# First batch of an attention + ELU MLP kernel: more places for softmax weights and raw weight words, earlier weight loads, v read once

## The chip, the cores and the metric

The kernel runs on one core of one Trainium2 chip. The metric is device microseconds of one execution.

## The reference

Eight batches of 12 heads with 448 positions and 64 channels go through attention with RMS-normalised q and k; the result, 3584 tokens of 768 channels, goes through a two-layer MLP with ELU and 2048 hidden channels. All in float32.

```python
q_n, k_n = rmsnorm(q, g_q), rmsnorm(k, g_k)
scores = q_n @ k_n.T / sqrt(64)
attn = exp(scores - max); attn = attn / (sum(attn) + 1e-09)
x = (attn @ v)                      # (8, 12, 448, 64) -> (3584, 768)
h = x @ w_in                        # (3584, 2048)
g = where(h > 0, h, exp(min(h, 0)) - 1)
return g @ w_out                    # (3584, 768)
```

## The kernel before

**Number format.** Products run on TensorE in float16. Each operand is split into a high and a low float16 part and scaled by powers of two; a product is three matmuls (high x high, high x low, low x high). For the weights this splitting is done once, on the chip, by `conv_in` (16 blocks f of `w_in`, results `whi[f]`, `wli[f]`) and `conv_out` (24 blocks of `w_out`, results `who[d]` and, through DRAM, `wl_d`). The power for v needs the largest absolute value of a batch's v: `scan_load` brings v in six pieces, `scan_max` (L139, DVE) takes the maxima, `v_steps` joins them.

**Tiling.** Two heads make a pair, six pairs a batch, 48 pairs in all. A pair has 7 chunks of 128 query rows (`T` counts chunks, 42 a batch, 336 in all). Per chunk: `s_mm` (L488, PE) computes scores into PSUM, `s_max` (L495, DVE) the row maxima, `s_exp` (L501, ACT), `s_z` (POOL), `s_rec` (DVE), then `s_hi` (L516, ACT) writes the softmax weights' high half into a buffer `p16`, `s_lo` (L522, DVE) the low half, and `s_tr` (L533) issues a transposing DMA `pt<-p` on the SP queue. `p16` has three buffers, so chunk T+3's `s_hi` waits until chunk T's transposes have landed. After its seven chunks a pair's `attend` (L544, PE) multiplies with v. `load_qk` (L307), `load_v` (L311, one buffer `vn`) and `qk_transpose` (L396) prepare later pairs on the same SP queue.

**MLP.** `mlp(b)` is 576 matmuls (L630, L644) per batch, spread over the half-steps of the next batch. So in the first batch no MLP matmul runs; the conversion of `w_in` fills that time, `w_out`'s begins in half-step 60 and ends in the second batch.

**Order.** The order is written out: a half-step `h` (two for a chunk, 84 for a batch, from -18 on) runs its loads first, then the chunk's softmax steps, then the tasks put down for it with `at`, then matmuls. Each engine works through its instructions in this order, and so does the SP queue, which issues every DMA; an SP instruction that waits holds back all behind it.

**Raw words.** `conv` starts a block f of `w_in` with `load` (L187, 768 KB), one half-step ahead of its h0, into one of two places of `raws`; `s_act` (L194, L195, ACT) reads it at h0+3, `s_sign` (L223, DVE) is the last reader at h0+7. Three blocks come every 14 half-steps, that is every pair (h0 = -10 + 14*((f-1)//3) + 0, 5 or 10). The blocks of `w_out` (512 KB) go through three places of the same tile.

Of the kernel before, what the change touches and what calls it, by code (L numbers as in the profile page):

```python
# [8 lines left out]
F32 = mybir.dt.float32  # L9
F16 = mybir.dt.float16  # L10
BF16 = mybir.dt.bfloat16
I32 = mybir.dt.int32
U32 = mybir.dt.uint32
# [6 lines left out]
B, H, S, D = 8, 12, 448, 64  # L20
NPAIR = H // 2
DM, DFF = 768, 2048
NC_, NF = DM // 128, DFF // 128
NJ = 2 * S // 128
NCHUNK = B * NPAIR * NJ
PB = NPAIR * NJ
WI_W, WO_W = DM, 32 * NF
# [5 lines left out]
def tile_attention_then_elu_mlp(ctx: ExitStack, tc: tile.TileContext, qk, v, v_scan, gg, w_in, w_out, out):  # L33
# [13 lines left out]
    nc = tc.nc  # L47
    nc.scalar.preload_act_table_set("natural_log_exp_and_others")

    const = ctx.enter_context(tc.tile_pool(name="const", bufs=1))  # L50
    dram = ctx.enter_context(tc.tile_pool(name="dram", bufs=1, space=DRAM))
    psum = ctx.enter_context(tc.tile_pool(name="psum", bufs=1, space=PSUM))
    pool = ctx.enter_context(tc.tile_pool(name="pool", bufs=1))
# [9 lines left out]
    def t_mo():  # L63
        return pst("mo", 3)
# [7 lines left out]
        out=neg, in0=ident, scalar1=-1.0, scalar2=None, op0=ALU.mult  # L72
# [3 lines left out]
        out=ident, in0=ident, scalar1=2.0**UP, scalar2=None, op0=ALU.mult  # L76
# [3 lines left out]
    eps = const.tile([128, 1], F32, name="eps")  # L80
    nc.vector.memset(eps, 1e-6)

    wl_d = [dram.tile([128, 128, NF], F16, name=f"wl_d{d}") for d in range(NC_)]

    whi = [const.tile([128, NC_, 128], F16, name=f"whi{f}") for f in range(NF)]
    wli = [const.tile([128, NC_, 128], F16, name=f"wli{f}") for f in range(NF)]
    who = [const.tile([128, 128, NF], F16, name=f"who{d}") for d in range(NC_)]
    NX = 9
    xs = [const.tile([128, 2, S], F16, name=f"x{i}") for i in range(NX)]
    gts = [const.tile([128, 2, S], F16, name=f"g{f}") for f in range(NF)]  # L90

    raws = const.tile([128, 2 * 2 * WI_W], U32, name="raws")
    wts = const.tile([128, 2 * WI_W], F32, name="wts")
    w32s = const.tile([128, 3 * WI_W], F32, name="w32s")

    def room(all, width, i):
        n = all.shape[1] // width
        return all[:, i % n * width : i % n * width + width]  # L100

    def small(name, w=1, dt=F32, bufs=2):
        return pool.tile([128, w], dt, tag=name, name=name, bufs=bufs)
# [3 lines left out]
    def upper(t):  # L107

        return t.bitcast(BF16).rearrange("p (n w) -> p n w", w=2)[:, :, 1]

    def column_sums(parts, bank):


        for i, a in enumerate(parts + [tiny]):
            nc.tensor.matmul(bank[:, S:], ones, a, start=i == 0, stop=i == len(parts))

    def largest(bank, e):
        nc.vector.tensor_reduce(out=e, in_=bank[:, S:], axis=AX.X, op=ALU.max)  # L118
        return e
# [3 lines left out]
    def ibits(dst, src, s1, op0, s2, op1):  # L123
        nc.vector.tensor_scalar(
            out=dst.bitcast(I32), in0=src.bitcast(I32), scalar1=s1, scalar2=s2, op0=op0, op1=op1
        )

    E = 1 << 23

    scans, mvs = {}, {}  # L130

    def scan_load(b, i):
        raw = scans[b, i] = pool.tile([128, VSW], F32, tag="e", name="vscan", bufs=3)
        nc.sync.dma_start(out=raw, in_=v_scan[b][:, i * VSW : (i + 1) * VSW])

# [30 lines left out]
    def on_pe(fn):  # L166

        late.add(fn)
        return fn
# [6 lines left out]
    def conv(src, i, width, acol, rows, parts, own=True):  # L176

        raw = room(raws, 2 * width, i).rearrange("p (n w) -> p n w", w=2)

        t, w = room(wts, width, i), room(w32s, width, i if width == WI_W else i + 2)
        ws = bank = None

        def load():
            nc.sync.dma_start(  # L187
                out=raw, in_=src[i].bitcast(U32).rearrange("p (n w) -> p n w", w=2)
            )

        def s_act():


            nc.scalar.activation(t, raw[:, :, 1].bitcast(F32), AF.Abs, scale=2.0**-112)  # L194
            nc.scalar.activation(w.bitcast(I32), raw[:, :, 0], AF.Copy, scale=2.0**-29)  # L195

        def s_shift():
            nc.vector.tensor_scalar(  # L198
                out=t.bitcast(I32), in0=t.bitcast(I32), scalar1=3, scalar2=None,
                op0=ALU.logical_shift_left,  # L200
            )

        def s_add():
            nc.gpsimd.tensor_tensor(
                out=w.bitcast(I32), in0=t.bitcast(I32), in1=w.bitcast(I32), op=ALU.add
            )

        def s_sums():
            nonlocal bank
            bank = t_mo() if own else av  # L210
            column_sums([upper(t[:, a : a + 64]) for a in range(0, width, 64)], bank)

        def s_scale():
            nonlocal ws
            e = largest(bank, acol if rows is None else small("mx"))
            ws = small("ws")

            ibits(ws, e, POWER, ALU.bitwise_xor, POWER, ALU.bitwise_and)
            if rows is not None:
                ibits(acol, e[rows], POWER, ALU.bitwise_and, 0, ALU.bitwise_or)  # L220

        def s_sign():
            nc.vector.scalar_tensor_tensor(  # L223
                out=w.bitcast(U32), in0=raw[:, :, 1], scalar=0x80000000, in1=w.bitcast(U32),
                op0=ALU.bitwise_and, op1=ALU.bitwise_or,
            )

        steps = [
            (0 if (width, i) == (WO_W, 1) else -1, load), (3, s_act), (4, s_shift), (5, s_add), (6, on_pe(s_sums)), (7, s_sign),
            (8, s_scale),  # L230
        ]
        for h, fn in parts:
            step = lambda fn=fn: fn(w, ws)
            steps.append((h, on_pe(step) if fn in late else step))
        return steps

    def conv_in(f):
        hi, lo = (t[f].rearrange("p c n -> p (c n)") for t in (whi, wli))
        half = [slice(0, 384), slice(384, 768)]
        dgw = None  # L240
        pss = [None, None]

        def s_diag(w, ws):
            nonlocal dgw
            dgw = pool.tile([128, 128], F32, tag="dgw", name="dgw", bufs=2)
            nc.scalar.activation(dgw, ident, AF.Copy, scale=ws)

        def s_high(w, ws):
            nc.gpsimd.tensor_scalar(
                out=hi, in0=w, scalar1=ws, scalar2=2.0**UP, op0=ALU.mult, op1=ALU.mult  # L250
            )

        def s_low(w, ws):
            for i, c in enumerate(half):
                pss[i] = t_mo()
                nc.tensor.matmul(pss[i][:, :384], dgw, w[:, c], start=True, stop=False)
                nc.tensor.matmul(pss[i][:, :384], neg, hi[:, c], start=False, stop=True)

        def s_out(i):
            nc.scalar.activation(lo[:, half[i]], pss[i][:, :384], AF.Copy)  # L260

        return conv(
            w_in, f, WI_W, a_in[:, f : f + 1], None,
            [(9, s_diag), (9, s_high), (11, on_pe(s_low)), (12, lambda w, ws: s_out(0)),
             (13, lambda w, ws: s_out(1))],
        )
# [31 lines left out]

    nat, vn, vt, qkt, pts, pss, p16s, stats = ({} for _ in range(8))
    st1, sqs, t16s = {}, {}, {}
    vscale, mscale, vpow = {}, {}, {}

# [2 lines left out]
        nc.sync.dma_start(out=nat[p].rearrange("p t j d -> p (t j) d"), in_=qk[p // NPAIR, p % NPAIR])  # L307

    def load_v(p):
        vn[p] = pool.tile([128, 4, 2, D], F32, tag="vn", name="vn", bufs=1)  # L310
        nc.sync.dma_start(out=vn[p], in_=v[p // NPAIR, p % NPAIR])  # L311

# [199 lines left out]
        nc.vector.reciprocal(out=st[:, 2:3], in_=st[:, 1:2])  # L512

    def s_hi(T):
        p16 = p16s[T] = pool.tile([128, 2 * S], F16, tag="p16", name="p16", bufs=3)
        nc.scalar.activation(p16[:, :S], pss[T][:, :S], AF.Copy, scale=stats[T][:, 2:3])  # L516

    def s_lo(T):
# [143 lines left out]
    def run_tasks(h, kind):  # L662
        for fn, args in tasks.get(h, []):
            if kind == (0 if fn in (load_qk, load_v, scan_load) else 2 if fn in late else 1):
                fn(*args)
# [24 lines left out]
    for b in range(B):  # L690
        h0 = HB * (b - 1) + HP * 2 if b else -5
        for i in range(VSC):
            at(h0 + 2 * i, scan_load, b, i)
            at(h0 + 2 * i + 3, scan_max, b, i)
        steps_at(h0 + (15 if b else 13), v_steps(b))
        at(HB * (b + 1), m_scale, b)
# [23 lines left out]
    for h in range(H0, LAST):  # L720
        T, odd = divmod(h, 2)
        run_tasks(h, 0)
        ok = lambda t: 0 <= t < NCHUNK
        if odd:
            if ok(T):
                s_exp(T)
            if ok(T - 1):
                s_rec(T - 1)
            if ok(T - 2):
                s_lo(T - 2)  # L730
        else:
            if ok(T):
                s_max(T)
            if ok(T - 1):
                s_z(T - 1)
            if ok(T - 2):
                s_hi(T - 2)

            for t in (T - 4, T - 3):
                if ok(t) and (t % NJ == 0) == (t == T - 4):  # L740
                    s_tr(t)
        run_tasks(h, 1)
        want = int(max(0, (h + 1 - START)) * RATE)
        n = max(0, want - done)
        mm = []
        p, r = divmod(h, HP)
# [15 lines left out]
    h = LAST - 1  # L762
# [49 lines left out]
```

## Time and profile before

| | |
|---|---|
| median of 3 runs | 1323.66 us (1322.05 to 1326.17) |
| profiled execution, its time | 1321.52 us |
| its span | 1319.7 us |
| mean granted TensorE clock | 0.957 |
| busy: PE, DVE, ACT, POOL | 1202.7, 897.0, 820.8, 672.4 us |

The profile's page cuts the span into 40 slices of 33 us and gives busy tenths for each engine, the granted TensorE clock (PEclk) and the busy share of the 16 DMA engines:

```profile
PE   3665558879999999999999999999999999999998
PEclk9777768989999999999999999999999999999999
DMA  7899998879878787888878877879687877764011
```

TensorE is at 9 tenths from the tenth slice on; the first slices are the first batch, and the second batch's start.

### The profile page before, as it was taken

The numbers are of one execution on the slowest core, as the hardware profiler recorded it, in microseconds if no ns is written. First come the engines' busy times: TensorE is split into PE (matmuls) and PEld (weight loads), VectorE is DVE, ScalarE is ACT, GpSimd is POOL, SyncE is SP. The second block draws the span as 40 slices with busy tenths as digits, with TensorE's granted clock in tenths as the row PEclk, the third lists the DMA queues.
The fourth block names the chain that finished last, engine by engine and source line by source line (L and its number), as shares of the span: only waits on it lengthen the run. The fifth ranks groups of instructions, "written<-read, shape, count | busy, mean of one in ns | idle before, by whom it ended". The sixth has DMA issues, their size and how long they took to land.

```text
span 1319.7 us, 22020 instructions
## 1 busy us (share of the span) xinstructions
PE 1202.7 (91%) x6976; PEld 723.1 (55%) x6976; DVE 897.0 (68%) x2257; ACT 820.8 (62%) x1761; POOL 672.4 (51%) x915
## 2 busy tenths in 40 slices
PE   3665558879999999999999999999999999999998
PEld 1322224436755675566655765577556755666576
DVE  7776788988668756885588657865687568842310
ACT  5767767776667657675577657756676567742310
POOL 5776798888445544544455345543454445421100
PEclk9777768989999999999999999999999999999999
DMA  7899998879878787888878877879687877764011
GB/s 236 195 233 223 201 203 189 209 205 204 199 140 194 163 187 151 178 165 189 173 153 177 190 172 147 187 171 193 144 190 163 189 150 154 152 135 110 1 46 60
DMA packets 491013, 221.76 MB, mean 168 GB/s; under 512 B 451856, under 2 KB 467344, under 8 KB 490896
## 3 DMA queue, kind: packets, MB, share of 16 engines
q1 hardware_dynamic: 490896, 220.35, 75.6%
q8 instruction: 55, 0.90, 0.3%
q14 instruction: 62, 0.51, 0.1%
HBM read 96.01 MB, written 14.16 MB: 83 GB/s over the span
## 4 chain that ended last, share of the span: by engine, by line
PE 67%; DMA 4%; DVE 4%; POOL 2%; issue 2%; ACT 2%; SPq 0%; ACTq 0%; POOLq 0%
PE mo L644 32%; PE mo L630 22%; PE s L488 7%; PE av L544 6%; DMA pt<-p 2%; DMA vscan<-in_v_scan 1%; DVE p L522 1%; POOL e L571 1%; POOL t L381 1%; DVE st L495 1%; DVE mv L139 0%; DVE e L577 0%; ACT p L516 0%; DVE wts L198 0%; ACT t L367 0%
## 5 line engine op out<-in xcount | busy, mean ns | idle before, releaser
L630 PE MATMUL mo<-x,whi 128*128 128x448 f16 x1536 | 425.8, 354 | 1.5 <-DVE e L577 1.5
L644 PE MATMUL mo<-g,who 128*128 128x448 f16 x1536 | 422.5, 352 | 0.0
L495 DVE TENSOR_REDUCE st<-s 128x1 f32<-128x448 f32 x336 | 208.1, 619 | 205.5 <-PE s L488 205.3
L522 DVE SCALAR_TENSOR_TENSOR p<-s,st,p 128x384 f16<-128x384 f32 (+1 forms) x672 | 266.4, 437 | 34.7 <-ACT p L516 33.2
L516 ACT ACTIVATE p<-s,st 128x448 f16<-128x448 f32 x336 | 213.1, 634 | 120.7 <-DMA pt<-p 95.3
L644 PE MATMUL mo<-g,wls 128*128 128x448 f16 x768 | 272.0, 354 | 0.0
L630 PE MATMUL mo<-x,wli 128*128 128x448 f16 x768 | 271.8, 354 | 0.0
L644 PEld LDWEIGHTS <-who 128*128 128x128 f16 x1536 | 221.9, 144 | 72.3
L505 POOL TENSOR_SCALAR st<-st 128x1 f32<-128x1 f32 x336 | 78.6, 234 | 350.7 <-ACT s L501 333.5
L501 ACT ACTIVATE s<-s,st 128x448 f32<-128x448 f32 x336 | 203.8, 607 | 74.0 <-DVE st L495 64.6
L488 PE MATMUL s<-qkt 128*128 128x448 f16 (+1 forms) x768 | 191.4, 372 | 58.9 <-DVE p L522 30.7
L630 PEld LDWEIGHTS <-whi 128*128 128x128 f16 x1536 | 150.6, 98 | 139.6 <-issue 4.4
L571 POOL TENSOR_SCALAR e<-e,isc 128x448 f32<-128x448 f32 x128 | 94.1, 735 | 179.5 <-ACT e L568 177.7
L644 PEld LDWEIGHTS <-wls 128*128 128x128 f16 x768 | 111.5, 145 | 42.1 <-issue 7.5
L488 PEld LDWEIGHTS <-qkt 128*128 128x128 f16 (+1 forms) x768 | 61.3, 102 | 131.6 <-DVE p L522 52.2
L544 PE MATMUL av<-pt,vt 128*64 128x448 f16 x1056 | 114.6, 366 | 5.2 <-DVE mx L118 4.3
L585 DVE SCALAR_TENSOR_TENSOR g<-e,gsc,g 128x448 f16<-128x448 f32 x128 | 100.8, 788 | 24.4 <-ACT g L582 24.3
L630 PEld LDWEIGHTS <-wli 128*128 128x128 f16 x768 | 75.2, 98 | 74.5 <-issue 8.1
L582 ACT ACTIVATE g<-e,gsc 128x448 f16<-128x448 f32 x128 | 85.4, 667 | 44.9 <-DVE e L577 44.1
L568 ACT ACTIVATE e<-mo,sc 128x448 f32<-128x448 f32 x128 | 80.4, 628 | 52.3 <-PE mo L630 33.1
L381 POOL TENSOR_TENSOR t<-nat,t 128x896 f16<-128x896 f32 x48 | 92.7, 1931 | 4.8 <-ACT t L367 1.1
L577 DVE SCALAR_TENSOR_TENSOR e<-e,mo 128x448 f32<-128x448 f32 x128 | 78.2, 611 | 23.9 <-POOL e L571 19.3
(84 smaller groups left out, 1330.0 us busy)
## 6 DMA issues: line engine op xcount, KB each, us to landing
wls<-wl_d SPq DMA_DIRECT2D x48, 512.0 KB, 3.9
nat<-in_qk SPq DMA_DIRECT2D x48, 448.0 KB, 3.7
raws<-in_w_in SPq DMA_DIRECT2D x16, 768.0 KB, 5.5
vn<-in_v SPq DMA_DIRECT2D x48, 256.0 KB, 3.7
raws<-in_w_out SPq DMA_DIRECT2D x24, 512.0 KB, 4.2
vscan<-in_v_scan SPq DMA_DIRECT2D x48, 224.0 KB, 3.0
out<-y SPq DMA_DIRECT2D x48, 224.0 KB, 3.2
pt<-p SPq DMA_TRANSPOSE x384, 3.2
```

The costliest lines, as they stand in the source:

```text
L381: nc.gpsimd.tensor_tensor(out=t[:, 2], in0=twice(nat[p][:, 1]), in1=t[:, 1], op=ALU.subtract)
L488: nc.tensor.matmul(ps[r0 : r0 + n, :S], lhs, qq[:, t, h * S : h * S + S], start=(t == 1), stop=(t == 2),)
L495: nc.vector.tensor_reduce(out=st[:, 0:1], in_=pss[T][:, :S], axis=AX.X, op=ALU.max, negate=True)
L501: nc.scalar.activation(ps, ps, AF.Exp, bias=st[:, 0:1], accum_out=st[:, 1:2])
L516: nc.scalar.activation(p16[:, :S], pss[T][:, :S], AF.Copy, scale=stats[T][:, 2:3])
L522: nc.vector.scalar_tensor_tensor(out=p16[:, o : o + z - a], in0=ps[:, a:z], scalar=r, in1=p16[:, a:z], op0=ALU.mult, op1=ALU.subtract,)
L544: nc.tensor.matmul(av[64 * h : 64 * h + 64, :S], vt[p][:, j % 4, h, i], pt[h][:, j, :], start=(k == 0), stop=(k == len(terms) - 1),)
L571: nc.gpsimd.tensor_scalar(out=e, in0=e, scalar1=-1.0, scalar2=isc, op0=ALU.add, op1=ALU.mult)
L582: nc.scalar.activation(g[:, 0], e, AF.Copy, scale=gsc)
L585: nc.vector.scalar_tensor_tensor(out=g[:, 1], in0=e, scalar=gsc, in1=g[:, 0], op0=ALU.mult, op1=ALU.subtract)
L630: nc.tensor.matmul(ph[:, :S], w[:, c, :], x[:, r, :], start=(c == 0 and i == 0), stop=last)
L644: nc.tensor.matmul(py[:, :S], w, g[:, r, :], start=(f == 0 and i == 0), stop=last)
```

## The change

- The scan of the first batch reads v in the layout that `attend` needs: `scan_load` brings pair i's v (256 KB) into `vfirst[i]`, which lies in the MLP's later `g` tiles (`gall`), and keeps it; `load_v` issues nothing for the first six pairs. The separate scan loads (6 x 224 KB) of batch 0 are gone.
- `s_hi` of the first 42 chunks uses eight places, `pfirst`, in the other half of `gall`, instead of three pool buffers.
- `conv_in` has six places for raw words: the two of `raws` and four in `whos`, the tile that `who` is now part of. Its load is issued 1 half-step ahead of h0 for block 2, 4 for block 3 and 7 for the later ones. (Blocks 0 and 1 have their own table and stay.)

```diff
+    whos = const.tile([128, NC_ * 128 * NF], F16, name="whos")
+    who = [t.rearrange("p (n f) -> p n f", f=NF) for t in cols(whos, NC_)]
...
+    gall = const.tile([128, NF * 2 * S], F16, name="gall")
+    gts = [t.rearrange("p (i s) -> p i s", i=2) for t in cols(gall, NF)]
+    vfirst = cols(gall[:, : NPAIR * 1024].bitcast(F32), NPAIR)
+    pfirst = cols(gall, NF)[8:]
...
+    raw_in = cols(raws, 2) + cols(whos.bitcast(U32), 4)
...
     def scan_load(b, i):
+        if b == 0:
+            scans[b, i] = vfirst[i]
+            vn[i] = vfirst[i].rearrange("p (j h d) -> p j h d", j=4, h=2)
+            nc.sync.dma_start(out=vn[i], in_=v[0, i])
+            return
...
-        raw = room(raws, 2 * width, i).rearrange("p (n w) -> p n w", w=2)
+        raw = raw_in[i % len(raw_in)] if width == WI_W else room(raws, 2 * width, i)
+        raw = raw.rearrange("p (n w) -> p n w", w=2)
...
-            (0 if (width, i) == (WO_W, 1) else -1, load), (3, s_act), (4, s_shift), ...
+            (-(1, 4, 7)[min(max(i - 2, 0), 2)] if width == WI_W else 0 if i == 1 else -1, load), (3, s_act), (4, s_shift), ...
...
     def load_v(p):
+        if p < NPAIR:
+            return
...
     def s_hi(T):
+        if T < PB:
+            p16 = p16s[T] = pfirst[T % len(pfirst)]
+        else:
+            p16 = p16s[T] = pool.tile([128, 2 * S], F16, tag="p16", name="p16", bufs=3)
```

On the compute engines the instructions stand as before, with other tiles. What moves is the SP queue. At the program's start, before (`raws` is a place for raw words, `vscan` a piece of the scan, `vn` a pair's v, `nat` a pair's q and k, `qkt<-t` their transposes):

```order
L187 DMA raws<-in_w_in 128x1536
L134 DMA vscan<-in_v_scan 128x448
L307 DMA nat<-in_qk 128x896
L134 DMA vscan<-in_v_scan 128x448
L311 DMA vn<-in_v 128x512
L134 DMA vscan<-in_v_scan 128x448
L187 DMA raws<-in_w_in 128x1536
L134 DMA vscan<-in_v_scan 128x448 x2
L187 DMA raws<-in_w_in 128x1536
L134 DMA vscan<-in_v_scan 128x448
L396 DMA_TRANSPOSE qkt<-t_308 128x7x128 x2
```

The same place after (`whos` holds raw words, `gall` pairs' v):

```order
L205 DMA whos<-in_w_in 128x1536
L148 DMA gall<-in_v 128x512
L205 DMA whos<-in_w_in 128x1536
L325 DMA nat<-in_qk 128x896
L148 DMA gall<-in_v 128x512
L205 DMA whos<-in_w_in 128x1536
L148 DMA gall<-in_v 128x512 x2
L205 DMA whos<-in_w_in 128x1536
L148 DMA gall<-in_v 128x512 x2
L416 DMA_TRANSPOSE qkt<-t_283 128x7x128 x2
```

Four blocks of raw words instead of three now stand ahead of the second pair's transposes, the second and third of them earlier among the loads of v; the piecewise scan and the first `vn` are gone.

The end of the fourth pair (pair 3) on the SP queue, before (`pt<-p` are the softmax weights' transposes; the first two of a pair wait for the PE's `attend` of the pair ahead, whose `pt` buffers they take):

```order
L396 DMA_TRANSPOSE qkt<-t_1068 128x7x128 x2
L307 DMA nat<-in_qk 128x896
L533 DMA_TRANSPOSE pt<-p_1122 128x7x128
L533 DMA_TRANSPOSE pt<-p_1148 128x7x128
L396 DMA_TRANSPOSE qkt<-t_1068 128x7x128
L187 DMA raws<-in_w_in 128x1536
L533 DMA_TRANSPOSE pt<-p_1222 128x7x128
L311 DMA vn<-in_v 128x512
L533 DMA_TRANSPOSE pt<-p_1255 128x7x128
L187 DMA raws<-in_w_in 128x1536
```

And after:

```order
L416 DMA_TRANSPOSE qkt<-t_1015 128x7x128 x2
L205 DMA whos<-in_w_in 128x1536
L325 DMA nat<-in_qk 128x896
L556 DMA_TRANSPOSE pt<-gall 128x7x128 x2
L416 DMA_TRANSPOSE qkt<-t_1015 128x7x128
L556 DMA_TRANSPOSE pt<-gall 128x7x128 x2
```

The raw words that stood behind the two blocked transposes and the third `qkt` now stand ahead of them, the `vn` load is gone, and no further load of `w_in` follows in this stretch.

More of the change, by code (lines that the diff above doesn't have):

```diff
@@ L81, in tile_attention_then_elu_mlp, with cols @@
     nc.vector.memset(eps, 1e-6)
+    def cols(t, n):
+        w = t.shape[1] // n
+        return [t[:, i * w : i * w + w] for i in range(n)]
     wl_d = [dram.tile([128, 128, NF], F16, name=f"wl_d{d}") for d in range(NC_)]
@@ L86, in tile_attention_then_elu_mlp @@
     wli = [const.tile([128, NC_, 128], F16, name=f"wli{f}") for f in range(NF)]
-    who = [const.tile([128, 128, NF], F16, name=f"who{d}") for d in range(NC_)]
+    whos = const.tile([128, NC_ * 128 * NF], F16, name="whos")
+    who = [t.rearrange("p (n f) -> p n f", f=NF) for t in cols(whos, NC_)]
     NX = 9
     xs = [const.tile([128, 2, S], F16, name=f"x{i}") for i in range(NX)]
-    gts = [const.tile([128, 2, S], F16, name=f"g{f}") for f in range(NF)]
+    gall = const.tile([128, NF * 2 * S], F16, name="gall")
+    gts = [t.rearrange("p (i s) -> p i s", i=2) for t in cols(gall, NF)]
+    vfirst = cols(gall[:, : NPAIR * 1024].bitcast(F32), NPAIR)
+    pfirst = cols(gall, NF)[8:]
     raws = const.tile([128, 2 * 2 * WI_W], U32, name="raws")
@@ L128, in tile_attention_then_elu_mlp @@
     E = 1 << 23
-    scans, mvs = {}, {}
+    scans, mvs, vn = {}, {}, {}
     def scan_load(b, i):
+        if b == 0:
[3 more added lines that the diff above has]
+            return
         raw = scans[b, i] = pool.tile([128, VSW], F32, tag="e", name="vscan", bufs=3)
@@ L228, in conv @@
         steps = [
-            (0 if (width, i) == (WO_W, 1) else -1, load), (3, s_act), (4, s_shift), (5, s_add), (6, on_pe(s_sums)), (7, s_sign),
+            (-(1, 4, 7)[min(max(i - 2, 0), 2)] if width == WI_W else 0 if i == 1 else -1, load), (3, s_act), (4, s_shift), (5, s_add), (6, on_pe(s_sums)), (7, s_sign),
             (8, s_scale),
@@ L297, in conv_out @@
         )
-    nat, vn, vt, qkt, pts, pss, p16s, stats = ({} for _ in range(8))
+    nat, vt, qkt, pts, pss, p16s, stats = ({} for _ in range(7))
     st1, sqs, t16s = {}, {}, {}
@@ L514, in s_hi @@
     def s_hi(T):
-        p16 = p16s[T] = pool.tile([128, 2 * S], F16, tag="p16", name="p16", bufs=3)
+        if T < PB:
+            p16 = p16s[T] = pfirst[T % len(pfirst)]
+        else:
+            p16 = p16s[T] = pool.tile([128, 2 * S], F16, tag="p16", name="p16", bufs=3)
         nc.scalar.activation(p16[:, :S], pss[T][:, :S], AF.Copy, scale=stats[T][:, 2:3])
```

## The prediction

> **What bounds the kernel now.** I read the page's slices first (shown above): TensorE is full from the tenth slice on, so only what shortens the first 300 us can shorten the run. Then busy time by stretches. I cut them at every seventh row maximum (L495), so each stretch is one pair of heads; that work is the same in each, as the first two rows, of L495 alone, show for the first and the last (x7, one for each chunk). The other rows are the six pairs of the first batch, two pairs of the second batch, and one of the steady part. Columns: length, busy us and instructions of PE, PEld, DVE, ACT, POOL, then granted clock, DMA busy share, GB/s.
>
> ```profile
> 24.00:48.00 24.00, 4.30 (x7) 0.84 0.87 229
> 153.50:180.00 26.50, 4.25 (x7) 0.63 0.92 216
> ...
> 24.00:48.00 24.00, 15.29 (x80) 7.47 (x78) 20.54 (x50) 17.96 (x39) 16.07 (x16) 0.84 0.87 229
> 48.00:74.90 26.90, 17.23 (x95) 8.13 (x95) 18.73 (x48) 19.43 (x43) 22.37 (x23) 0.75 0.83 195
> 74.90:101.90 27.00, 16.63 (x95) 7.81 (x95) 21.54 (x53) 19.50 (x43) 19.68 (x20) 0.75 0.99 246
> 101.90:129.20 27.30, 16.80 (x98) 8.14 (x98) 18.09 (x51) 19.64 (x44) 20.15 (x20) 0.75 0.91 203
> 129.20:153.50 24.30, 16.19 (x98) 8.29 (x98) 16.93 (x49) 19.32 (x46) 17.69 (x19) 0.78 0.88 192
> 153.50:180.00 26.50, 11.22 (x74) 4.64 (x74) 21.53 (x55) 18.61 (x41) 24.00 (x27) 0.63 0.92 216
> 209.60:239.70 30.10, 26.35 (x166) 13.41 (x165) 27.57 (x67) 23.82 (x50) 26.07 (x29) 0.89 0.85 178
> 239.70:275.50 35.80, 27.82 (x176) 13.51 (x174) 31.54 (x74) 24.57 (x51) 28.43 (x33) 0.95 0.83 205
> 330.50:353.60 23.10, 23.10 (x135) 16.34 (x134) 13.12 (x35) 12.74 (x29) 9.65 (x18) 1.00 0.91 205
> ```
>
> In the steady part PE is busy 23.10 of 23.10 us. In the first batch no engine is: in pair 3 (101.90 on) the busiest, POOL, has 20.15 of 27.30, and the DMA engines 0.91. The time goes into waits that all engines share, because each works in a fixed order. The waits of ACT over the six pairs (total us, times, longest):
>
> ```profile
> ACT wts L194 <- DMA raws<-in_w_in: 14.1, 4, 4.1
> ACT p L516 <- DMA pt<-p: 9.0, 7, 2.1
> ACT x L551 <- PE av L544: 5.9, 4, 2.0
> ```
>
> The first two are what the change is at. One of the four waits for raw words, in order of time: the queue's issues, then what each engine did next, with its idle time in brackets.
>
> ```profile
> 114.68 0.33 SPq L307 DMA_DIRECT2D nat<-in_qk  x1
> 118.19 2.56 SPq L533 DMA_TRANSPOSE pt<-p  x2
> 120.81 1.29 SPq L396 DMA_TRANSPOSE qkt<-t  x1
> 122.19 0.53 SPq L187 DMA_DIRECT2D raws<-in_w_in  x1
> 123.80 0.55 PE L488 MATMUL s<-qkt 128*128 128x448 f16 x2 [1.80 <-DMA qkt<-t]
> 127.81 0.89 ACT L194 ACTIVATE wts<-raws 128x768 f32<-128x768 f32 x1 [4.11 <-DMA raws<-in_w_in]
> 128.73 0.56 DVE L198 TENSOR_SCALAR wts<-wts 128x768 int32<-128x768 int32 x1 [3.46 <-ACT wts L194]
> 130.19 0.19 POOL L505 TENSOR_SCALAR st<-st 128x1 f32<-128x1 f32 x1 [4.11 <-ACT s L501]
> 130.83 1.65 PE L256 MATMUL mo<-w32s,dgw 128*128 128x384 f32 x2 [4.58 <-ACT dgw L246]
> ```
>
> The load leaves the queue only at 122.19, behind two transposes that wait for `attend` (the queue stands from 115.01 to 118.19); ACT stands 4.11 us for it, and DVE, POOL and PE stand with it. So this wait is on the path, whatever the shares of busy time say.
>
> **The change, part by part.**
>
> *Raw words early, six places.* Loads of block 4 and later move six half-steps ahead. A pair has 14 half-steps, so at 27 us for a pair that is some 11 us, against waits of at most 4.1. A place comes free with the sign step of the block six earlier, 28 half-steps ahead of the new h0, so the queue never waits for DVE there. The four waits fall, one in each of pairs 0 to 3:
>
> ```profile
> 46.60 0.90 ACT L194 ACTIVATE wts<-raws 128x768 f32<-128x768 f32 x1 [2.33 <-DMA raws<-in_w_in]
> ...
> ACT wts L194 <- DMA raws<-in_w_in: 3.7, 1, 3.7
> ...
> ACT wts L194 <- DMA raws<-in_w_in: 4.0, 1, 4.0
> ...
> ACT wts L194 <- DMA raws<-in_w_in: 4.1, 1, 4.1
> ```
>
> What comes next once they are gone? Pair 4 (129.20 on) answers: by then `w_in` is nearly in, it has no such wait, still three p16 buffers, and takes 24.30 us. Pairs 1 to 3 take 26.90 + 27.00 + 27.30 = 81.2; three like pair 4 would take 72.9. I take that difference, 8.3 us. The waits on raw words and p16 in those three pairs are 11.8 + 4.3 = 16.1 (4.3 is 9.0 less pair 0's 1.08 and the 3.6 of pairs 4 and 5, rows below), so about half (0.52) of what ACT waits comes back and the rest is taken by what is late next: PE's wait for `qkt` (1.80 above), ACT's for `attend` (5.9 in all), and POOL, busy 22.37 in pair 1.
>
> *Eight places for p16.* With three, chunk T+3 waits for chunk T's transposes to land; with eight, a chunk waits for the transposes of the one eight earlier, long landed. That the eight places are parts of one tile, which the MLP's g shares, adds no wait: in the built program each waits for its own place alone, and the MLP writes there after the last of them. Rows of the wait in pair 0, and in pairs 4 and 5 together:
>
> ```profile
> 40.58 0.64 ACT L516 ACTIVATE p<-s,st 128x448 f16<-128x448 f32 x1 [1.08 <-DMA pt<-p]
> ...
> ACT p L516 <- DMA pt<-p: 3.6, 2, 2.1
> ```
>
> At the same 0.52, pair 0 (2.33 + 1.08 = 3.41) gives 1.8, pairs 4 and 5 give 1.9. Between nothing and 9.0 for all p16 waits I stay at that half because SP issues the transposes in the same order and no sooner.
>
> *v once.* Six loads of 224 KB go; the six of 256 KB move to the start. At the densest row, 246 GB/s at 0.99, a scan load is 0.23 MB and so 0.9 us of all DMA engines, 5.6 us for six. That is DMA time, not path time: I price it at nothing because it lies beside the engines' work, and it is what pays for the heavier start. If the DMA engines are the true bound, it is the whole gain (a rival below). The scan itself (L139) reads 512 columns instead of 448: 0.61 x 512/448 is 0.70, six times 0.09 is 0.5 us more on DVE.
>
> ```profile
> 22.22 0.61 DVE L139 TENSOR_REDUCE mv<-vscan 128x1 f32<-128x448 f32 x1
> 24.98 0.62 DVE L139 TENSOR_REDUCE mv<-vscan 128x1 f32<-128x448 f32 x1 [0.31 <-DMA vscan<-in_v_scan]
> ```
>
> *The heavier start.* Between the first transposes and those of pair 1, SP now issues one block of raw words more (0.79 MB) and 0.2 MB more of v for the scan, less 0.26 MB of the old first `vn`; two blocks stand earlier among v's pieces. DVE takes these in a fixed order and waited only 0.31 us for one before. Net 0.7 MB is 2.9 us at 246 GB/s; hidden it costs nothing (at 24.00 to 48.00 the engines have 0.13 of 24 us free, 3.1 us), unhidden twice that, when the second block delays a piece too: 0 to 6. I take 2.0, nearer the free row, because what is late here is one piece or two, not all.
>
> *The queue.* Six issues of `vn` and the wait for its one buffer go from between the transposes; nothing waits behind the moved loads that did not wait before, except that three of four pairs' third `qkt` transpose now follows 768 KB of data rather than preceding it. The blocked queue gives that load its time: the 3.18 us up to 118.19.
>
> *The clock.* PE's pair of fp32 matmuls (L256) took 1.65 us after the stall above; a row 10 us earlier, after a short gap, is
>
> ```profile
> 120.12 0.91 PE L256 MATMUL mo<-w32s,dgw 128*128 128x384 f32 x2 [0.56 <-ACT dgw L246]
> ```
>
> so a stall also slows what follows, by 0.74 us here. The Trainium skill, "TensorE: Matmul & The Clock Gate", Part 1, says that PE falls to half its clock after an idle window of about 3.4 us; by that rule removing gaps like the 4.58 us one would give this back in three pairs, and the sum would be 2.2 us better. The row bears out the size, but pair 4, without the long stall, still has a granted clock of 0.78 against 0.75, so I add nothing for it.
>
> *Later.* From chunk 42 on, places and loads are as before. Pairs 6 to 9 are held by DVE and POOL (27.57 of 30.10, 31.54 of 35.80), then by PE; whatever the first batch gains moves all of that forward unchanged.
>
> *Sum.* -8.3 - 1.8 - 1.9 + 0.5 + 2.0 = -9.5 us. The profiled execution took 1321.52, the median of the runs is 2.1 above; 1323.66 - 9.5 is about 1314.
>
> **Rivals.**
>
> 1. All of the waits come back: 14.1 + 9.0 less 0.5 is 22.6, 1301. For it: all four engines stand together in the rows of the stall. Against: pair 4, and POOL's 22.37 us in pair 1, under which that pair can't go; it would need 26.90 - 5.1 = 21.8.
> 2. The DMA engines are the bound, and the waits for raw words only show it: 0.99 in pair 2. Then places and earlier issues move nothing, and only the scan loads' work goes: at most 5.6 us, of which the start keeps 2, so about 1320, no difference that can be told. Against: 0.83 in pair 1, which stalls 3.7 us all the same.
> 3. Slower: the early blocks stand ahead of transposes that PE needs. 0.79 MB at 246 GB/s is 3.2 us a block. If in each of pairs 0 to 4 one such block delays the third `qkt` transpose, on which PE's next scores wait, that is up to 16 us against a gain of 12.0; with 2.5 of costs, 1330. It decides when more than 9.5 / 5 = 1.9 us of each block is not over when the queue frees. The Trainium skill, "DMA: Bandwidth & Descriptors", section on queues, rings and completion order, speaks for it: each DMA engine takes descriptors in ring order, so a transpose can't pass a load. Against: SP stands at `attend` behind the load, and the landing times over 30 to 200 us, where loads stood among transposes already, are mild:
>
> ```profile
> raws<-in_w_in SPq DMA_DIRECT2D x11, 768.0 KB, 5.4
> ...
> pt<-p SPq DMA_TRANSPOSE x50, 4.1
> ```
>
> **How the numbers follow.** The likeliest, half of the waits, with its unknowns (start 0 to 6, share 0.35 to 0.75 of 23.1, not both at their ends): 1308 to 1319, chance 0.66. Rival 1 and what lies toward it, 0.12. Rival 2, 0.14. Rival 3, 0.08. A run of this kernel can tell about 0.3%, 4 us, from no change. So faster 0.78, same 0.14, slower 0.08. The range goes from 1303, most of the way to rival 1, to 1321, which takes in rival 2.
>
> **What would show it.** In the profile after: no wait of ACT on raw words in 24 to 180 us and none on `pt<-p`; pairs 1 to 3 at 24 to 25 us; the sixth pair's end near 170 instead of 180; pairs 6 to 9 and the steady 23.1 us as before. If the waits are gone and pairs 1 to 3 still take 27 us at a DMA share near 1, rival 2 holds. If PE's wait on `qkt<-t` grows by over 2 us a pair, rival 3. If DVE waits over 4 us for the first v's, the start was priced too low.

## The result, and the profile after

The changed kernel takes 1316.34 us (median; 1315.52 to 1317.2) against 1324.7 before: ratio 0.9936, 95% interval 0.9917 to 0.9954. In a second comparison the same kernel gave 0.993 (0.9913 to 0.9948). The forecast was 1314 with 1303 to 1321, faster.

The pairs of the first batch, two of the second and a steady one, cut as before at every seventh row maximum (columns: length, busy us and instructions of PE, PEld, DVE, ACT, POOL, granted clock, DMA busy share, GB/s):

```profile
24.00:48.00 24.00, 15.67 (x82) 8.16 (x81) 19.48 (x51) 20.24 (x44) 16.55 (x18) 0.86 0.97 256
48.00:71.70 23.70, 14.23 (x95) 6.78 (x94) 18.50 (x47) 19.14 (x42) 21.50 (x22) 0.85 0.88 193
71.70:96.00 24.30, 16.79 (x98) 8.29 (x98) 20.32 (x54) 19.70 (x43) 21.20 (x22) 0.78 1.10 261
96.00:118.40 22.40, 15.08 (x97) 7.75 (x95) 19.33 (x52) 18.96 (x43) 19.33 (x19) 0.78 0.99 226
118.40:141.20 22.80, 14.68 (x99) 7.36 (x98) 18.00 (x49) 17.99 (x42) 18.87 (x21) 0.85 0.77 166
141.20:167.80 26.60, 10.67 (x81) 4.60 (x77) 21.98 (x55) 18.46 (x41) 23.60 (x26) 0.67 1.00 221
197.20:227.00 29.80, 24.34 (x169) 12.63 (x167) 27.41 (x67) 23.67 (x50) 25.98 (x29) 1.00 0.97 186
227.00:262.60 35.60, 27.40 (x173) 13.21 (x172) 31.52 (x73) 24.59 (x51) 28.39 (x33) 0.95 0.82 201
317.70:341.50 23.80, 23.50 (x136) 16.36 (x135) 13.31 (x36) 12.81 (x29) 9.59 (x18) 1.00 0.89 200
```

Pairs 1 to 4 are 3.2, 2.7, 4.9 and 1.5 us shorter, pairs 0 and 5 as long as before. Pair 5 ends at 167.8 instead of 180.0: 12.2 us. ACT's waits over the first batch, longest first:

```profile
ACT x L574 <- PE av L567: 8.5, 4, 2.8
ACT s L521 <- DVE st L515: 7.6, 9, 2.7
ACT wli L278 <- PE mo L275: 6.0, 8, 1.7
```

Both waits the change was at, 14.1 and 9.0 us, are gone; what is late next is `attend`, the row maxima and the conversion's matmuls, 5.9, 1.8 and 4.9 us before in rows of the same kind.

But the span falls only from 1319.7 to 1314.9, by 4.8. The other 7 us are lost again in the steady part (pair 12 to the last row maximum), which takes 844.6 us after and 837.4 before. These are two single executions. The one before was faster than its median (1321.52 against 1324.7), and the medians differ by 8.4, so the usual loss is nearer 4 us. PE's waits in the steady part, after and then before:

```profile
PE av L567 <- DVE mx L130: 7.1, 5, 1.6
PE av L567 <- DMA pt<-p: 1.6, 2, 1.3
PE s L508 <- DVE p L545: 1.5, 2, 1.0
```

```profile
PE av L544 <- DVE mx L118: 4.3, 4, 1.5
PE av L544 <- DMA pt<-p: 0.8, 1, 0.8
```

So the questions are which of the three parts gave the gain, and who takes it back.

### The profile page after: what moved, and what is told of

Its sections match the earlier page's. It is cut to its first block, busy times and chain, and to the rows that moved or that the text cites. A ratio compares the mean times of both kernels' runs of the same rounds, so it can differ in the third digit from the quotient of the medians.

```text
span 1314.9 us, 21982 instructions
## 1 busy us (share of the span) xinstructions
PE 1196.3 (91%) x6976; PEld 719.8 (55%) x6976; DVE 897.2 (68%) x2257; ACT 821.2 (62%) x1761; POOL 672.5 (51%) x915
## 4 chain that ended last, share of the span: by engine, by line
PE 66%; DMA 5%; ACT 3%; DVE 2%; issue 2%; POOL 2%; SPq 0%; ACTq 0%; POOLq 0%
PE mo L667 31%; PE mo L653 22%; PE s L508 7%; PE av L567 7%; DMA pt<-p 4%; DMA vscan<-in_v_scan 1%; POOL t L401 1%; POOL e L594 1%; ACT p L539 1%; ACT s L521 0%; DVE st L515 0%; DVE p L545 0%; ACT t L387 0%; DVE mv L156 0%; DMA raws<-in_w_out 0%
## 5 line engine op out<-in xcount | busy, mean ns | idle before, releaser
L667 PE MATMUL mo<-gall,whos 128*128 128x448 f16 x1536 | 422.5, 352 | 0.0
L667 PE MATMUL mo<-gall,wls 128*128 128x448 f16 x768 | 272.0, 354 | 0.0
L667 PEld LDWEIGHTS <-whos 128*128 128x128 f16 x1536 | 221.9, 144 | 72.3
L545 DVE SCALAR_TENSOR_TENSOR p<-s,st,p 128x384 f16<-128x384 f32 x588 | 233.1, 438 | 38.3 <-ACT p L539 37.7
L525 POOL TENSOR_SCALAR st<-st 128x1 f32<-128x1 f32 x336 | 82.1, 244 | 346.0 <-ACT s L521 331.4
L539 ACT ACTIVATE p<-s,st 128x448 f16<-128x448 f32 x294 | 185.8, 632 | 113.8 <-DMA pt<-p 98.7
L608 DVE SCALAR_TENSOR_TENSOR gall<-e,gsc,gall 128x448 f16<-128x448 f32 x128 | 101.0, 789 | 25.1 <-ACT gall L605 24.8
L605 ACT ACTIVATE gall<-e,gsc 128x448 f16<-128x448 f32 x128 | 85.3, 666 | 45.0 <-DVE e L600 44.6
```

Of the source, the lines that this page charges most:

```text
L545: nc.vector.scalar_tensor_tensor(out=p16[:, o : o + z - a], in0=ps[:, a:z], scalar=r, in1=p16[:, a:z], op0=ALU.mult, op1=ALU.subtract,)
L605: nc.scalar.activation(g[:, 0], e, AF.Copy, scale=gsc)
L608: nc.vector.scalar_tensor_tensor(out=g[:, 1], in0=e, scalar=gsc, in1=g[:, 0], op0=ALU.mult, op1=ALU.subtract)
L667: nc.tensor.matmul(py[:, :S], w, g[:, r, :], start=(f == 0 and i == 0), stop=last)
```

## The experiments

All ratios are to the kernel before. Lengths, in us, from each kernel's profile, one execution each. The kernels with one part alone and the one with "loads not moved" have the joint tiles `gall` and `whos` too.

| kernel | pairs 0 to 5 | pairs 6 to 11 | steady part | ratio (95% interval) |
|---|---|---|---|---|
| before | 156.0 | 173.6 | 837.4 | |
| changed kernel | 143.8 | 173.7 | 844.6 | 0.9936 (0.9917 to 0.9954) |
| same, again | 143.3 | 172.7 | 841.6 | 0.993 (0.9913 to 0.9948) |
| p16 places alone | 155.2 | 172.5 | 840.5 | 1.001 (0.9997 to 1.0022) |
| raw words alone | 151.1 | 172.8 | 838.4 | 0.9938 (0.9923 to 0.9953) |
| v once alone | 154.6 | 173.9 | 836.0 | 0.9987 (0.9976 to 0.9997) |
| joint tiles alone | 156.4 | 173.9 | 838.7 | 1.0003 (0.9992 to 1.0015) |
| six places, loads not moved | 155.6 | 174.6 | 837.1 | 1.0003 (0.9991 to 1.0015) |
| all but p16 places | 148.8 | 172.5 | 839.6 | 0.9936 (0.992 to 0.9952) |
| all but v once | 143.0 | 172.4 | 843.3 | 0.9918 (0.9901 to 0.9934) |
| all, v_steps earlier | 143.4 | 172.4 | 834.4 | 0.986 (0.984 to 0.9879) |
| the same without p16 places | 146.4 | 172.3 | 832.6 | 0.9893 (0.9877 to 0.9909) |
| before, v_steps earlier | 156.3 | 173.3 | 832.5 | 0.9966 (0.9952 to 0.9979) |
| all, v_steps earlier, conv_out later | 143.9 | 178.7 | 832.4 | 0.99 (0.9884 to 0.9916) |

**The raw words alone.** Kernel before with six places and early loads:

```diff
+        raw = raw_in[i % len(raw_in)] if width == WI_W else room(raws, 2 * width, i)
+            (-(1, 4, 7)[min(max(i - 2, 0), 2)] if width == WI_W else 0 if i == 1 else -1, load), ...
```

> The kernel before with six places for raw words and the early loads alone. Theory: pairs 1 to 3 take 24 to 25 us each instead of 26.9 to 27.3, the end of pair 5 comes 7 to 9 us earlier; the time falls by 5 to 9 us. Rival (DMA bound): the stalls move to p16 or to the qkt transposes and the time falls by less than 2 us.

1314.81 us, 8.5 less than before and as much as the full change. ACT has no wait on raw words left in its profile; its first two rows now are

```profile
ACT p L529 <- DMA pt<-p: 10.1, 7, 2.5
ACT x L564 <- PE av L557: 9.0, 4, 2.7
```

They were 9.0 and 5.9 before: little of the stall went over to p16, more of it to `attend` and to smaller waits. Pairs 1 and 3 (24.0, 24.9) came as expected; pair 2 stayed at 27.5, outside what was expected. The end of pair 5, at 175.0, lies outside it too: 5 us earlier, not 7 to 9. The time itself is within what was expected; the profiled execution was the slowest of five (1316.61) and shows only 4.9 of the 8.5 us.

**Six places, loads where they were.**

```diff
+        raw = raw_in[i % len(raw_in)] if width == WI_W else room(raws, 2 * width, i)
             (0 if (width, i) == (WO_W, 1) else -1, load), ...
```

> The kernel before with six places for raw words, but each load issued where it was, one half-step ahead of h0. Theory (the load is late because it stands in the queue behind the transposes that wait for attend): the four waits of ACT on raw words stay within 1 us of 2.3, 3.7, 4.0, 4.1 and the time within 2 us of before. Rival (the load is late because its place is not free): the waits shrink to less than half and most of the 8.5 us of raws_only comes with it.

```profile
ACT wts L207 <- DMA whos<-in_w_in: 14.4, 4, 4.0
ACT p L529 <- DMA pt<-p: 8.5, 8, 1.7
```

Nothing changed: 14.4 us in four waits, as 14.1 before. Free places do nothing by themselves; the earlier issue, which they make possible, does it all. Standing for `attend` is only part of what made the load late. In pairs 0 to 3 of the kernel before, the queue stood 0.1, 1.3, 2.7 and 3.2 us ahead of the two transposes; issuing these and the third `qkt` then took 4 us each time, and ACT could read the block 5.4 to 6.1 us after the load's issue.

**The p16 places alone.**

```diff
+        if T < PB:
+            p16 = p16s[T] = pfirst[T % len(pfirst)]
+        else:
             p16 = p16s[T] = pool.tile([128, 2 * S], F16, tag="p16", name="p16", bufs=3)
```

> The kernel before with eight places for the first batch's softmax weights; raw words and v as before. Theory (waits that all engines share): ACT's 9.0 us of waits on pt<-p in the first batch go, the four waits on raw words stay at 2 to 4 us each, and about half of the 9.0 comes back: 3 to 5 us less than before. Rival (the DMA engines are the bound and the waits only show it): no change within 2 us, and the waits on raw words grow by what the p16 waits lose.

No gain. The p16 waits are gone, and those on raw words are longer, one of them now 5.75 us:

```profile
ACT wts L207 <- DMA raws<-in_w_in: 17.7, 4, 5.8
...
76.32 0.89 ACT L207 ACTIVATE wts<-raws 128x768 f32<-128x768 f32 x1 [5.75 <-DMA raws<-in_w_in]
```

The time is the rival's; of its second sign, waits on raw words longer by the 9.0 us that p16 loses, only 3.6 came. The DMA engines as a bound aren't needed to explain it. In this longest wait, in pair 1, the load itself left later. The queue and ACT here, and then in the kernel before:

```profile
66.65 2.57 SPq L549 DMA_TRANSPOSE pt<-gall  x2
70.66 0.53 SPq L200 DMA_DIRECT2D raws<-in_w_in  x1
```

```profile
63.89 2.56 SPq L533 DMA_TRANSPOSE pt<-p  x2
67.89 0.53 SPq L187 DMA_DIRECT2D raws<-in_w_in  x1
73.49 0.89 ACT L194 ACTIVATE wts<-raws 128x768 f32<-128x768 f32 x1 [3.69 <-DMA raws<-in_w_in]
```

The queue stood for `attend` until 66.65 instead of 63.89, so the load left 2.8 us later and ACT got its block 2.8 us later; pair 1 takes 29.8 us instead of 26.9. Why `attend` came later there is not shown. Pairs 3 and 4 got shorter (25.5, 22.6), so the places gain there what pair 1 loses.

**v once alone, and the joint tiles alone.**

```diff
+        if b == 0:
+            scans[b, i] = vfirst[i]
+            nc.sync.dma_start(out=vn[i], in_=v[0, i])
+            return
```

> The kernel before with the first batch's v read once and kept. Theory: DMA time off the path, minus a start that is no heavier here (raw words as before): 0 to 2 us less. Rival (DMA bound): all of the DMA time of the six scan loads comes back, 4 to 6 us.

0.9987: 1.7 us, at the theory's end and far from the 4 to 6 of the DMA bound.

> The kernel before with the g tiles in one tile and the who tiles in one tile, nothing else: the same instructions, other addresses. In the two profiles the steady part (pairs 12 to 47 and their MLP) takes 837.5 us before and 844.6 after, so 7 of the 12.3 us of the first batch seem to be given back. If the joint tiles cause it: time 5 to 8 us over before, steady part near 845. If that is a difference between single executions: time within 2 us of before, steady part anywhere between 837 and 846.

No change, and a steady part of 838.7: the addresses of the joint tiles don't take anything back.

**The full change without one part.**

> The kernel after, but with three buffers for the softmax weights throughout. Theory A (the p16 places alone gave nothing, 1.001, because ACT's raw-word wait took over; beside the early raw words they give 3 to 7 us in the first batch and the full kernel is that much faster than this one): 1317 to 1321, pairs 2 and 3 near 26 us. Theory B (the p16 places give the run nothing in any company): 1312 to 1316, as the full kernel or faster.

> The kernel after, with v scanned and loaded separately as before. v alone took 1.3 to 1.7 us off. Theory A (parts add up): 1316 to 1318, the first batch's pairs together some 1.5 us longer than in the full kernel. Theory B (the DMA engines bound pairs 0 to 2 once the waits are gone): pair 2 with its six scan loads and pair 0 slower by 2 us or more, 1318 or over.

> The full kernel unchanged, for a second profile of its steady part (pairs 12 to 47): 844.6 us in the first against 836.0 to 840.5 in five others. If that is a difference between executions: 836 to 841 here, and the end of pair 5 again near 168. If the change causes it: 844 to 846.

Without p16's places (`bufs=3` throughout) the run takes 1315.15, as with them; theory B. Yet the first batch is 5 us longer, 3.6 of it in pair 2, where ACT stands for a buffer and the six scan loads of batch 1 pass (its waits in pair 2, and the pair's row):

```profile
ACT p L536 <- DMA pt<-p: 4.3, 2, 3.2
...
72.30:100.20 27.90, 16.16 (x97) 7.73 (x96) 22.19 (x53) 20.41 (x45) 20.67 (x22) 0.81 1.08 256
```

Without the v part (scan and loads separate) the first batch is as short, 143.0, and the time if anything lower (1312.45 against 1313.97), as neither theory had it: beside the others, v once gives nothing. The repeat of the full kernel has its steady part at 841.6, between the two values that were expected. Over all profiles without the v_steps edit, the four with p16's places have steady parts of 840.5 to 844.6, the six without 836.0 to 839.6. So the loss goes with p16's places, as far as one profile each can show (840.5 and 839.6 are close), and not with the joint tiles.

**Where part of it is lost: v_steps one half-step earlier.** In every batch, PE puts the sums for the scan's maximum into the PSUM bank `av` (L127), DVE takes the maximum (L130), and the next pair's `attend` needs the bank. In the full kernel:

```profile
562.78 0.22 PE L127 MATMUL av<-dg,ones 128*128 128x64 bf16 x2
...
566.22 0.62 DVE L515 TENSOR_REDUCE st<-s 128x1 f32<-128x448 f32 x1
566.75 0.22 DVE L130 TENSOR_REDUCE mx<-av 128x1 f32<-128x64 f32 x1
567.00 0.15 DVE L136 TENSOR_SCALAR p<-mx 128x1 int32<-128x1 int32 x1
...
567.02 2.24 PE L567 MATMUL av<-pt,vt 128*64 128x448 f16 x21 [1.59 <-DVE mx L130]
```

The sums are there at 563; DVE, working in order, comes to the maximum only at 566.75, and PE, nearly full otherwise, stands 1.59 us. This wait also tells the kernels apart. In the steady part it sums to 7.1, 7.2, 7.6 and 7.9 us in the four with p16's places (full, again, p16 alone, all but v once) and to 3.4 to 5.8 us in the six without. That is 2.5 us on average, against 4.6 us between the two groups' steady parts, so it is about half of the loss.

```diff
-        steps_at(h0 + (15 if b else 13), v_steps(b))
+        steps_at(h0 + (14 if b else 13), v_steps(b))
```

> The full kernel with the joining of the scan's maxima (v_steps) one half-step earlier in batches 1 to 7. In every profile PE stands 0.4 to 1.6 us in each batch before a pair's attend for the DVE maximum over the sums that v_steps puts in the same PSUM bank. Theory: with a half-step between them these waits go, the steady part falls to 833 to 836 us and the time by 3 to 8 us against the full kernel. Rival: DVE is behind anyway and the wait moves to the next instruction; no change within 2 us.

1304.51 us, 9.5 below the full kernel on the same chip, more than expected: the steady part falls from 841.6 to 834.4, and PE's waits in it are

```profile
PE s L508 <- DVE p L545: 1.3, 2, 1.0
PE av L567 <- DMA pt<-p: 0.7, 1, 0.7
```

No wait for the maximum is left, and the steady part is shorter by 7.2 us, the sum of these waits in the repeat of the full kernel. It is the best kernel of the study. The same edit alone and without p16's places:

> The kernel before with the earlier v_steps alone. Its profile shows 4.3 us of PE's waits for that maximum in the steady part, the full kernel's 7.1. Theory: about that much comes off, 1317 to 1320; on the full kernel it was 9.5 us, so if the change made those waits longer this gain is smaller. Rival: the gain has nothing to do with the change, 9 to 10 us here too, 1313 to 1315.

> The version with the earlier v_steps, with three buffers for the softmax weights throughout. So far the eight places end pair 5 about 5 us earlier (167.3 and 167.8 against 172.8 without them) and the steady part is 2 to 5 us longer (841.6 and 844.6 against 839.6), so the run gains nothing. Theory A (what they gain is lost at PE's waits for v_steps' maximum): with those waits gone the eight places are worth their 5 us, and this one takes 1308 to 1311, ratio 0.989 to 0.991. Theory B (it is lost elsewhere): 1303 to 1306, ratio 0.985 to 0.987, as with them, and the steady part 2 us or more shorter than 834.4.

On the kernel before it is worth 0.34% (1317.28), about its 4.3 us of waits, half of what it gives on the full kernel. Without p16's places it ends at 0.9893, against 0.986 with them: about 4 us, theory A by the time, though the two intervals touch and come from two chips. The profiles say less. With p16's places the first batch is 3.0 us shorter and the steady part still 1.8 longer (834.4 against 832.6), and the two profiled executions are 1.1 us apart. So with the wait for the maximum out of the way p16's places gain something at the end; how much of their gain in the first batch arrives is not settled.

**Another step moved, a miss.**

```diff
-            [(9, s_mult), (10, s_high), (11, s_low), (12, s_store)], own=i < WO_OWN,
+            [(9, s_mult), (11, s_high), (12, s_low), (13, s_store)], own=i < WO_OWN,
```

> The version with the earlier v_steps, and in conv_out the high halves, low halves and store one half-step later (10, 11, 12 to 11, 12, 13). In pair 5 and in the second batch ACT waits about 2 us for POOL's multiplication in each of several blocks (ACT on POOL w32s: 5.8 us in 24 to 175 us of the full kernel, 14.5 us over the first 260 us of before). Theory: these waits are on the path as those on raw words were, half of them comes back, pairs 5 to 9 together 3 to 8 us shorter, 1297 to 1302. Rival (POOL and DVE bound these pairs): within 2 us of 1304.5.

4 us slower than without it by the medians, and slower by the intervals too (0.9884 to 0.9916 against 0.984 to 0.9879): neither the theory nor the rival. Pairs 6 to 11 take 6.3 us more. ACT's waits for POOL (16.5 us from 140 to 300 us in the kernel with the earlier v_steps, first row) are gone, but POOL now waits for ACT and the raw words of `w_out` come too late (the other rows):

```profile
ACT whos L303 <- POOL w32s L298: 16.5, 10, 2.6
```

```profile
POOL w32s L307 <- ACT whos L303: 9.2, 8, 2.1
...
ACT wts L212 <- DMA raws<-in_w_out: 7.7, 4, 3.5
```

## Why the prediction was right, and where it was not

*Pairs 1 to 3*, -8.3 forecast from pair 4 as it was: -10.8 measured with all parts, -4.8 with the raw words alone (24.0, 27.5, 24.9 against 81.2 in all). The mechanism was right: the waits went, and the pairs got shorter by a part of them. The size was a little low, probably because pair 4, the measure, still had its own p16 wait of 2.1 us; it takes 22.80 after the change. The blocked queue, to which the prediction put the load's lateness, is a part of it only.

*p16 at half of its waits.* Right only in company: -5 us of first batch beside the early raw words, -0.8 alone. The term for pairs 4 and 5, -1.9, measured -1.4. I priced two waits of one engine by one share, as if each came back by itself; with p16 alone, the waits on raw words grew by 3.6 us as its own 9.0 went.

*The heavier start, 2.0, and pair 0, -1.8.* Pair 0 stayed at 24.0 us and began at 24.0 as before: the two cancel, or both are small. For small: pair 0 takes 23.9 with p16 alone and 24.5 with the raw words alone. The first v's were late by little:

```profile
24.96 0.69 DVE L156 TENSOR_REDUCE mv<-gall 128x1 f32<-128x512 f32 x1 [0.39 <-DMA gall<-in_v]
27.54 0.69 DVE L156 TENSOR_REDUCE mv<-gall 128x1 f32<-128x512 f32 x1 [1.34 <-DMA gall<-in_v]
```

The 0.09 us more for a scan of 512 columns is 0.07 to 0.08 here.

*v once at nothing.* Close: 1.7 us alone, nothing beside the others.

*"Later": all of it moves forward unchanged.* This step failed. The first batch gave 12.2 us where the sum had 9.5 net, and 4 to 7 us were lost again in the steady part. I had read PE's 23.10 of 23.10 in one pair as a bound for all; about once a batch PE stands up to 1.6 us for DVE. A sum that was too small and a loss that it lacked met at 1316: that the forecast of 1314 came so near is in part luck.

*Rival 2, the DMA engines as bound:* the share went up to 1.10 in pair 2 and the pair still got shorter, so 0.99 was no ceiling. *Rival 3, transposes behind early loads:* PE's wait for `qkt` over the first batch, before and after:

```profile
PE s L488 <- DMA qkt<-t: 8.9, 4, 2.9
```

```profile
PE s L508 <- DMA qkt<-t: 11.3, 5, 2.9
```

2.4 us more over the batch, not 16. The Trainium skill, "DMA: Bandwidth & Descriptors", "Queues, rings and completion order", says that each DMA engine consumes descriptors in ring order, though a later one may finish its write before an earlier one. The traces agree with the prediction's use of it. In the profiles before and after, 303 and 315 transposes were issued while a plain DMA was still in flight, and none landed ahead of it. In the first 200 us a transpose behind a block of `w_in` landed 4.7 us after its issue (median, in both), and one with no plain DMA in flight after 3.0. So the delay is real, about 1.7 us for such a transpose, and PE's wait shows only a part of it.

*The clock.* The granted clock rose from 0.75 to 0.85, 0.78 and 0.78 in pairs 1 to 3. The Trainium skill, "TensorE: Matmul & The Clock Gate", Part 1, puts the clock at half after an idle window of about 3.4 us; fewer long gaps would then raise it. The rows agree in sign; what the rise is worth was not measured.

What stays open is how p16's places, used only in the first 42 chunks, lengthen PE's waits in later batches; the instructions there are the same. Shown is only where about half of the loss arises, by the edit that removes these waits.

## What to carry to other kernels

When every engine and the DMA queue work in a written order, look for the load that leaves late before looking for a buffer that is missing, and issue it ahead of the instructions in the queue that hold it back. Price two waits on one engine together, since freeing one may lengthen the other. And before counting a gain at the front of a run as a gain of the run, look for small waits of the engine that bounds the rest: here waits of up to 1.6 us a batch, removed by moving a step half a chunk's time, were worth 9.5 us, about as much as the whole change.

## What the hardware showed that was not expected

The DMA busy share is no utilisation: it read 1.10 in a pair in which 261 GB/s moved, and 0.99 in the same pair before at 246. In the 40 slices of 0.6 us of that pair after the change, those that read 0.9 or more moved anything from 42 to 421 GB/s:

```profile
DMA  8999999129999998999989977999999999959999
GB/s 293 394 280 304 279 310 177 8 87 272 290 273 374 364 327 319 285 282 259 186 273 184 283 121 202 374 395 421 369 374 220 218 243 283 42 126 364 278 228 81
```

A share is the time that packets took, summed over 16 engines; that packets which wait count as busy would explain a sum over 1, but no run tests it. A reading near 1 does not say that no more can move.
